# Routing attention and a gelu feed-forward block: another way to load and turn the first pair of heads

## The chip, the cores and the metric

The kernel runs on one core of a Trainium2 chip. The core has TensorE (matmuls, called PE in the profile, with its weight loads as PEld), VectorE (DVE), ScalarE (ACT), GpSimd (POOL), and SyncE (SP), which here only issues transfers; ACT can issue transfers too. The metric is device time in microseconds (us), the median of several runs. Lower is better.

## What is computed

The reference is an attention in which a query sees only the keys of its own cluster, followed by a feed-forward block. Its core:

```python
# q, k, v: (4, 8, 768, 64); centroids: (8, 16, 64)
q_assign = np.argmax(np.einsum('bhsd,hcd->bhsc', q_n, c_n), axis=-1)
k_assign = np.argmax(np.einsum('bhsd,hcd->bhsc', k_n, c_n), axis=-1)
mask = q_assign[:, :, :, None] == k_assign[:, :, None, :]
scores = scale * np.matmul(q, k.transpose(0, 1, 3, 2))
scores = np.where(mask, scores, -1000000000.0)
...                                   # softmax over the keys -> attn
attn_out = np.matmul(attn, v)
...                                   # (B, H, S, D) -> x of (B*S, H*D) = (3072, 512)
h = x @ w_in                          # (512, 2048)
g = h * (1.0 / (1.0 + np.exp(-1.702 * h)))
return (g @ w_out).astype(np.float32)
```

The index `_n` means divided by its own length. For an argmax over centroids the length of q or k does not matter, so the kernel divides only the centroids.

## The kernel before

The attention goes over 16 pairs of heads, (batch, two heads) each. With two heads of 64 features, one pair fills the 128 partitions. A pair `p` has q (`w = 0`) and k (`w = 1`). Each must lie in SBUF with the features on the partitions, as a tile `T[p, w]` of 128 x 768, before scores can be made. The function `prep_turn` makes `T`, `prep_near` multiplies it with the centroids (`cT`, both heads of the pair side by side in 32 columns), `prep_assign` finds the best centroid of every token, and then a mask is added to the scores as a second small matmul (`part`): for pairs from 1 on, one row of codes per head, which `prep_spread` sends through DRAM into `rows_of`; for pair 0, one-hot rows `hots`, made on the chip by `prep_hot`.

Pair 0 and the other pairs take different ways through these functions:

- Loading (`load_qk`). Pair 0: one transfer per head, token `128 j + p` on partition `p`, each piece the 64 features of a token, 256 bytes. Other pairs: a head is loaded in two transfers of 32 features each, pieces of 128 bytes, 32 partitions per transfer, so that 32 x 32 blocks of the tile need only be transposed in place. All are issued by SP.
- Turning (`prep_turn`). Pair 0: twelve transposes on TensorE (L329) by an identity matrix into PSUM, three to a bank, and four copies by ACT (L334). Other pairs: one block transpose of 128 x 768 on VectorE for each of q and k (L322).
- Products with the centroids (`prep_near`). Pair 0: four matmuls of 384 columns, each into 32 partitions of one PSUM bank (L355), then a copy by ACT to SBUF (L361). Other pairs: eight matmuls of 192 columns (L343), which stay in PSUM.
- Assignment (`prep_assign`). Pair 0: three transposes on TensorE (L369). Other pairs: one block transpose on VectorE inside the PSUM bank (L366). Then, for both, a maximum over the 16 centroids (L375), a comparison (L378), a product with a rank (L381). Pair 0 takes another maximum (`code`, L387) and compares it with the ranks, which gives the one-hot tile `hot` (L389).
- Mask operands. Pair 0 (`prep_hot`): twelve small transposes on TensorE (L433), then `hots[0]` is copied from PSUM by VectorE (L438) and `hots[1]` by ACT, as `FAR * x - FAR` (L440).

The order on each engine is the order of the program text, which is written out by hand (a manual schedule). TensorE's filler matmuls on the identity, `keep_busy(n)` at L291, whose result nobody reads, stand between the steps of the start: six before the centroids are transposed (L298), three after `prep_near(0)`, six after the scores of the first two units, four after `prep_hot`. The main loop then goes over steps `t` of two units: scores (L467), mask (L481 for pair 0, L490 for others), exponentials on ACT (L498), sums on GpSimd (L516), values (L532). In step 0, behind the first scores, stand `prep(0, 6)`, which is `prep_hot(0)`, and then the first `part`. Pair 1's q is transposed by VectorE between `prep_assign(0)` and `prep_hot(0)` in VectorE's order, its k right after.

On SP's queue, in order: q and k of pair 0 (four transfers), q of pair 1 (four, L134), v of pair 0 (L144), k of pair 1 (four), a block of weights (L170), q of pair 2, and so on. The tiles of q and k come from a pool of three buffers (`inp`), so k of pair 1 has to wait until q of pair 0 has been turned. Eight completion semaphores serve the transfers in rotation, so a transfer also waits until the one that had its semaphore before has landed. ACT issues the load of the centroids (L151) and no other transfer until the end of the kernel.

After the attention come the feed-forward block (lines from 760 on) and its stores, which the change does not touch.

Of the kernel before, what the change touches and what calls it, by code (L numbers as in the profile page):

```python
# [9 lines left out]
BF16 = mybir.dt.bfloat16  # L10
# [28 lines left out]
def fast(  # L39
# [26 lines left out]
    nc = tc.nc  # L66
# [46 lines left out]
    def bank():  # L113
        return ps_m.tile([P, 512], FP32, name="m")

    def short():
        return tmp.tile([P, HALF], FP32, name="short")
# [4 lines left out]
    def load_qk(p, w):  # L122
        t = inp.tile([P, NJ, 2, D], FP32, name="in")
        b, hp = divmod(p, HP)
        for a in range(2):
            src = (q, k)[w][b, 2 * hp + a]
            if p == 0:
                nc.sync.dma_start(
                    out=t[:, :, a, :],
                    in_=src.rearrange("(j p) d -> p j d", p=P))  # L130
                continue
            for e in range(D // SQ):
                r = a * D + e * SQ
                nc.sync.dma_start(  # L134
                    out=t[r:r + SQ].rearrange("p j a d -> p (j a d)")
                    .rearrange("p (n d) -> p n d", d=SQ),
                    in_=src.rearrange("(n t) d -> t n d", t=SQ)[
                        :, :, e * SQ:(e + 1) * SQ])
        qk_in[p, w] = t
# [177 lines left out]
    def prep_turn(p, i):  # L317
        w, h = divmod(i, 2)
        if h == 0:
            T[p, w] = pairs.tile([P, S], FP32, name=f"T{w}")  # L320
            if p > 0:
                nc.vector.transpose(  # L322
                    out=T[p, w],
                    in_=qk_in[p, w].rearrange("p j a d -> p (j a d)"))
        if p > 0:
            return
        ps = bank()
        for n in range(NH):
            nc.tensor.transpose(out=ps[:, n * P:(n + 1) * P],  # L329
                                in_=qk_in[p, w][:, h * NH + n].rearrange(  # L330
                                    "p a d -> p (a d)"),
                                identity=ident)
        dst = T[p, w][:, h * HALF:(h + 1) * HALF]
        nc.scalar.copy(dst, ps[:, 0:HALF])  # L334

    def prep_near(p):


        ps = bank()
        if p > 0:  # L340
            for w in range(2):
                for r in range(0, P, SQ):
                    nc.tensor.matmul(  # L343
                        out=ps[r:r + SQ, w * NJ * SQ:(w + 1) * NJ * SQ]
                        .rearrange("p (j t) -> p j t", t=SQ),
                        lhsT=cT[:, p % HP].rearrange("p a c -> p (a c)"),
                        rhs=T[p, w].rearrange("d (j t) -> d j t", t=P)[
                            :, :, r:r + SQ],
                        start=True, stop=True)
            sT[p] = ps  # L350
            return
        for w in range(2):
            for h in range(2):
                r = 32 * (2 * w + h)
                nc.tensor.matmul(  # L355
                    out=ps[r:r + 32, 0:HALF],
                    lhsT=cT[:, p % HP].rearrange("p a c -> p (a c)"),
                    rhs=T[p, w][:, h * HALF:(h + 1) * HALF],
                    start=True, stop=True)
        sT[p] = short()  # L360
        nc.scalar.copy(sT[p], ps[:, 0:HALF])  # L361

    def prep_assign(p):
        ps = bank()
        if p > 0:
            nc.vector.transpose(out=ps[:, 0:HALF], in_=sT.pop(p)[:, 0:HALF])  # L366
        else:
            for n in range(NH):
                nc.tensor.transpose(out=ps[:, n * P:(n + 1) * P],  # L369
                                    in_=sT[p][:, n * P:(n + 1) * P],  # L370
                                    identity=ident)
        n = NJ * 4
        sc = ps[:, 0:n * NC].rearrange("p (n c) -> p n c", c=NC)
        best = asg.tile([P, n], FP32, name="best", bufs=1)
        nc.vector.tensor_reduce(out=best, in_=sc, axis=AX.X, op=ALU.max)  # L375
        eq = sc if p > 0 else short().bitcast(BF16)[:, 0:n * NC].rearrange(
            "p (n c) -> p n c", c=NC)
        nc.vector.tensor_tensor(  # L378
            out=eq, in0=sc, in1=best[:, :, None].broadcast_to((P, n, NC)),
            op=ALU.is_equal)  # L380
        nc.vector.tensor_tensor(  # L381
            out=eq, in0=eq, in1=rank[:, None, :].broadcast_to((P, n, NC)),
            op=ALU.mult)
# [15 lines left out]
        turned = ps[:, HALF:HALF + SQ]  # L399
        nc.vector.transpose(out=turned, in_=codes)  # L400
        row = code[p] = asg.tile([P, 2, SQ], BF16, name="row")
        nc.vector.tensor_copy(out=row[:, 0], in_=turned)
        nc.vector.scalar_tensor_tensor(
            out=row[:, 1], in0=turned, scalar=1.0 / CODE, in1=row[:, 0],
            op0=ALU.mult, op1=ALU.mult)
# [17 lines left out]
    def prep_hot(p):  # L423


        rows = slice(0, 2 * SQ)
        for w in range(2):
            hots[w] = hp1.tile([P, S], BF16, name=f"hots{w}")
            ps = bank().bitcast(BF16)
            for h in range(2):  # L430
                for n in range(NH):
                    at = (h * NH + n) * P
                    nc.tensor.transpose(  # L433
                        out=ps[rows, at:at + P],
                        in_=hot_w(w, h, n), identity=ident_h)
            dst = hots[w][rows, :]
            if w == 0:
                nc.vector.tensor_copy(out=dst, in_=ps[rows, 0:S])  # L438
            else:
                nc.scalar.activation(out=dst, in_=ps[rows, 0:S], func=AF.Copy,  # L440
                                     scale=FAR, bias=-FAR)

    def hot_w(w, h, n):
        j = ((n * 2 + w) * 2 + h) * 2
        return hot[:, j:j + 2, :].rearrange("p a c -> p (a c)")

    PREP = [lambda p, i=i: prep_turn(p, i) for i in range(4)]
# [1054 lines left out]
```

## Time and profile before

| | us |
|---|---|
| median of 3 runs (lowest to highest) | 911.01 (910.65 to 911.41) |
| the profiled execution, its own time | 910.43 |
| its span, first to last instruction | 908.5 |
| TensorE busy in the span | 888.4 |
| VectorE busy | 728.6 |
| GpSimd busy | 492.1 |
| ACT busy | 363.3 |

The page cuts the span into 40 slices of 22.7 us. Each digit is a busy share in tenths; the DMA row is the busy share of the 16 DMA engines, and GB/s what they moved:

```profile
PE   8999999999999999999999999999999999999994
DVE  4999999998899997998998556797556797557894
ACT  3777767777676773322111222112222112222110
PEclk9999999999999999999999999999999999999998
DMA  9465556666665210036213202322202322200323
```

The first slice is the only one but the last in which TensorE is not almost fully busy, and the one in which the transfers take the most of the DMA engines. A busy TensorE need not run at its peak: the page models the ends of matmuls. Engines other than TensorE may be idle without a cost.

### The profile page before, as it was taken

Reading aid. Unit: us, or ns where it says so; the run is one execution under the profiler, and the core shown is the slowest. Engines: PE = TensorE matmul, PEld = TensorE weight load, DVE = VectorE, ACT = ScalarE, POOL = GpSimd, SP = SyncE. Lnnn points to the kernel's source line nnn. Section 1 sums busy time; section 2 is a strip of 40 time slices with the busy share of each in tenths; the row PEclk is TensorE's granted clock in tenths of the full one; section 3 lists DMA queues with packets and bytes.
Section 4 is the critical chain, followed back from the end, with each engine's and each line's share of the span. In section 5 each row is a group of like instructions: output and inputs, shape, how many; then the busy total and the mean of one; then the engine's idle time right before and its main releaser. Section 6 shows DMA issues by size and latency. Waiting matters only on the chain.

```text
span 908.5 us, 17741 instructions
## 1 busy us (share of the span) xinstructions
PE 888.4 (98%) x6712; PEld 577.7 (64%) x6712; DVE 728.6 (80%) x1170; ACT 363.3 (40%) x816; POOL 492.1 (54%) x469
## 2 busy tenths in 40 slices
PE   8999999999999999999999999999999999999994
PEld 3344444444444445557996557997557997557994
DVE  4999999998899997998998556797556797557894
ACT  3777767777676773322111222112222112222110
POOL 5899989998999998693274221243221243220220
PEclk9999999999999999999999999999999999999998
DMA  9465556666665210036213202322202322200323
GB/s 176 117 131 107 102 119 129 146 136 132 132 132 122 85 43 18 0 117 232 70 53 109 48 1 70 103 74 90 48 1 70 105 70 93 47 1 1 105 75 69
DMA packets 178397, 78.97 MB, mean 87 GB/s; under 512 B 155272, under 2 KB 161536, under 8 KB 178304
## 3 DMA queue, kind: packets, MB, share of 16 engines
q1 hardware_dynamic: 176912, 77.53, 35.4%
q8 instruction: 55, 0.90, 0.5%
q10 hardware_dynamic: 1392, 0.23, 0.2%
q14 instruction: 38, 0.31, 0.1%
HBM read 61.03 MB, written 16.70 MB: 86 GB/s over the span
## 4 chain that ended last, share of the span: by engine, by line
PE 81%; DVE 9%; DMA 3%; issue 2%; SPq 2%; ACT 2%; POOL 0%; DVEq 0%; ACTq 0%
PE b L845 32%; PE b L895 23%; PE s L467 11%; PE o L532 9%; PE m L549 3%; PE s L490 2%; DVE G L593 2%; DMA raw<-in_moe_w_out_dram 2%; DVE E L593 1%; ACT A L498 1%; SPq L418 1%; DVE Tx L593 1%; PE m L343 1%; DMA line<-row 1%; DVE x L570 1%
## 5 line engine op out<-in xcount | busy, mean ns | idle before, releaser
L516 POOL TENSOR_TENSOR sum<-sum,A 128x384 f32<-128x384 f32 x252 | 264.0, 1082 | 35.8 <-ACT A L498 22.6
L836 DVE TENSOR_TENSOR G<-b,G 128x384 f32<-128x384 f32 x224 | 123.0, 556 | 99.2 <-PE b L845 89.4
L498 ACT ACTIVATE A<-s 128x768 f32<-128x768 f32 x192 | 144.7, 803 | 93.9 <-PE s L490 73.8
L593 POOL TENSOR_TENSOR Y<-y,Y 128x768 f32<-128x768 f32 x28 | 67.4, 2422 | 175.0 <-DVE y L836 151.0
L467 PE MATMUL s<-T,T 64*64 64x384 f32 x1536 | 144.5, 491 | 2.7 <-ACT A L498 0.9
L850 ACT ACTIVATE G<-G 128x384 f32<-128x384 f32 x128 | 66.3, 523 | 198.9 <-DVE G L836 197.6
L532 PE MATMUL o<-A,inv 64*64 64x384 f32 x1536 | 141.3, 483 | 0.0
L593 POOL TENSOR_TENSOR W<-w_in 128x256 f32<-128x256 f32 x32 | 23.6, 736 | 164.2 <-PE b L845 163.8
L593 DVE TENSOR_TENSOR G<-G 128x768 f32<-128x768 f32 (+1 forms) x92 | 104.1, 1156 | 0.0
L467 PEld LDWEIGHTS s<-T,T 64*64 64x64 f32 x1536 | 52.0, 132 | 79.1 <-ACT A L498 52.0
L845 PE MATMUL b<-Tx,w_in 128*128 128x384 f32 x256 | 93.0, 486 | 0.0
L845 PE MATMUL b<-x,W 128*128 128x384 f32 x256 | 93.0, 486 | 0.0
L845 PE MATMUL b<-x,w_in 128*128 128x384 f32 x256 | 88.6, 486 | 0.0
L532 PEld LDWEIGHTS o<-A,inv 64*64 64x64 f32 x1536 | 58.7, 133 | 38.2 <-issue 33.3
L845 PEld LDWEIGHTS b<-x,W 128*128 128x128 f32 x256 | 48.6, 190 | 33.9
L845 PEld LDWEIGHTS b<-Tx,w_in 128*128 128x128 f32 x256 | 48.6, 190 | 33.9
L845 PEld LDWEIGHTS b<-x,w_in 128*128 128x128 f32 x256 | 48.5, 190 | 33.5 <-issue 0.6
L895 PE MATMUL b<-G,w_out 128*128 128x192 f32 x320 | 55.9, 326 | 0.0
L895 PEld LDWEIGHTS b<-G,w_out 128*128 128x128 f32 x320 | 52.7, 190 | 1.1
L895 PE MATMUL b<-E,Wz 128*128 128x192 f32 x288 | 51.5, 328 | 1.4 <-DVE E L593 1.4
L895 PEld LDWEIGHTS b<-E,Wz 128*128 128x128 f32 x288 | 47.1, 190 | 3.4 <-POOL Wz L593 1.3
L845 PE MATMUL b<-Tx,W 128*128 128x384 f32 x128 | 46.6, 487 | 1.5 <-DVE Tx L593 1.5
(169 smaller groups left out, 1357.5 us busy)
## 6 DMA issues: line engine op xcount, KB each, us to landing
Wz<-kept_w SPq DMA_DIRECT2D x78, 256.0 KB
raw<-in_moe_w_in_dram SPq DMA_DIRECT2D x16, 512.0 KB
raw<-in_moe_w_out_dram SPq DMA_DIRECT2D x16, 512.0 KB
inv<-in_v_dram SPq DMA_DIRECT2D x16, 384.0 KB
in<-in_q_dram SPq DMA_DIRECT2D x60, 96.0 KB
in<-in_k_dram SPq DMA_DIRECT2D x60, 96.0 KB
kept<-x SPq DMA_DIRECT2D x24, 192.0 KB
x<-kept SPq DMA_DIRECT2D x24, 192.0 KB
```

The lines of the kernel that those rows point to most:

```text
L343: nc.tensor.matmul(out=ps[r:r + SQ, w * NJ * SQ:(w + 1) * NJ * SQ] .rearrange("p (j t) -> p j t", t=SQ), lhsT=cT[:, p % HP].rearrange("p a ...
L467: nc.tensor.matmul(out=ps[c:c + D, a, 0:HALF], lhsT=T[p, 1][rows, kt * P + c:kt * P + c + D], rhs=T[p, 0][rows, h * HALF:(h + 1) * HALF], ...
L490: nc.tensor.matmul(out=s_of[u][c:c + D, a, :], lhsT=rows_of[1, p % 2][rows, kt * P + c:kt * P + c + D], rhs=rows_of[0, p % 2][rows, h * HA ...
L498: nc.scalar.activation(out=A_of[u], in_=s_of.pop(u), func=AF.Exp, scale=SCALE)
L516: nc.gpsimd.tensor_tensor(out=sum_of[g][:, a], in0=(A_of[u - 1] if kt == 1 else sum_of[g])[:, a], in1=A_of[u][:, a], op=ALU.add)
L532: nc.tensor.matmul(out=o_of[g][a * D:(a + 1) * D, r, 0:HALF], lhsT=v_in[p][rows, a, kt, :], rhs=A[rows, a, :], start=(kt == 0), stop=(kt = ...
L549: nc.tensor.matmul(out=ps[a * D:(a + 1) * D, 0:HALF], lhsT=twos, rhs=sm[:, a, :], start=(i == 0), stop=(i == len(parts) - 1))
L593: engine.tensor_tensor(out=o, in0=a, in1=b, op=(ALU.add if op == "+" else ALU.subtract))
L836: nc.vector.tensor_tensor(out=o, in0=p, in1=a, op=ALU.add)
L845: nc.tensor.matmul(out=ps[:, 0:HALF], lhsT=a[:, c], rhs=x(c), start=(c == 0), stop=(c == 1))
L850: nc.scalar.activation(out=g, in_=g, func=AF.Gelu_apprx_sigmoid, scale=2.0)
L895: nc.tensor.matmul(out=ps, lhsT=A[n][:, f], rhs=M[n][:, f], start=start and f == 0, stop=(f == FQ - 1), skip_group_check=True)
```

## The change

For pair 0, the special way is taken out and the way of the other pairs is used:

- `load_qk` loads pair 0 in 128-byte pieces too, four transfers for q and four for k. Those of k are issued by ACT, those of q by SP.
- `prep_turn(0, .)` is one block transpose on VectorE for q and one for k.
- `prep_near(0)` is the eight matmuls of 192 columns, and their result stays in PSUM.
- `prep_assign(0)` transposes on VectorE inside the bank, and the comparison and the product with the rank are written to PSUM as 32-bit numbers instead of SBUF as bf16.
- `prep_hot` first makes all twelve transposes, then copies in two column halves: `hots[0]` by ACT, `hots[1]` by VectorE (before: `hots[0]` whole by VectorE, `hots[1]` whole by ACT). `hot_w` picks the columns in the order in which they now lie.

The fillers and the order of the steps are as before.

```diff
     def load_qk(p, w):
...
         for a in range(2):
             src = (q, k)[w][b, 2 * hp + a]
-            if p == 0:
-                nc.sync.dma_start(
-                    out=t[:, :, a, :],
-                    in_=src.rearrange("(j p) d -> p j d", p=P))
-                continue
             for e in range(D // SQ):
                 r = a * D + e * SQ
-                nc.sync.dma_start(
+                (nc.scalar if p == 0 and w else nc.sync).dma_start(
                     out=t[r:r + SQ].rearrange("p j a d -> p (j a d)")
                     .rearrange("p (n d) -> p n d", d=SQ),
...
     def prep_turn(p, i):
...
-            if p > 0:
-                nc.vector.transpose(
-                    out=T[p, w],
-                    in_=qk_in[p, w].rearrange("p j a d -> p (j a d)"))
-        if p > 0:
-            return
-        ps = bank()
-        for n in range(NH):
-            nc.tensor.transpose(out=ps[:, n * P:(n + 1) * P],
-                                in_=qk_in[p, w][:, h * NH + n].rearrange(
-                                    "p a d -> p (a d)"),
-                                identity=ident)
-        dst = T[p, w][:, h * HALF:(h + 1) * HALF]
-        nc.scalar.copy(dst, ps[:, 0:HALF])
+            nc.vector.transpose(
+                out=T[p, w],
+                in_=qk_in[p, w].rearrange("p j a d -> p (j a d)"))
...
     def prep_near(p):
...
-        for w in range(2):
-            for h in range(2):
-                r = 32 * (2 * w + h)
-                nc.tensor.matmul(
-                    out=ps[r:r + 32, 0:HALF],
-                    lhsT=cT[:, p % HP].rearrange("p a c -> p (a c)"),
-                    rhs=T[p, w][:, h * HALF:(h + 1) * HALF],
-                    start=True, stop=True)
-        sT[p] = short()
-        nc.scalar.copy(sT[p], ps[:, 0:HALF])
...
     def prep_assign(p):
         ps = bank()
-        if p > 0:
-            nc.vector.transpose(out=ps[:, 0:HALF], in_=sT.pop(p)[:, 0:HALF])
-        else:
-            for n in range(NH):
-                nc.tensor.transpose(out=ps[:, n * P:(n + 1) * P],
-                                    in_=sT[p][:, n * P:(n + 1) * P],
-                                    identity=ident)
+        nc.vector.transpose(out=ps[:, 0:HALF], in_=sT.pop(p)[:, 0:HALF])
...
-        eq = sc if p > 0 else short().bitcast(BF16)[:, 0:n * NC].rearrange(
-            "p (n c) -> p n c", c=NC)
+        eq = sc
...
     def prep_hot(p):
...
-            dst = hots[w][rows, :]
-            if w == 0:
-                nc.vector.tensor_copy(out=dst, in_=ps[rows, 0:S])
-            else:
-                nc.scalar.activation(out=dst, in_=ps[rows, 0:S], func=AF.Copy,
-                                     scale=FAR, bias=-FAR)
+            hot_ps[w] = ps
+        for h in range(2):
+            cols = slice(h * HALF, (h + 1) * HALF)
+            nc.scalar.copy(hots[0][rows, cols], hot_ps[0][rows, cols])
+            nc.vector.tensor_scalar(
+                out=hots[1][rows, cols], in0=hot_ps[1][rows, cols],
+                scalar1=FAR, scalar2=-FAR, op0=ALU.mult, op1=ALU.add)
 
     def hot_w(w, h, n):
-        j = ((n * 2 + w) * 2 + h) * 2
+        j = (w * NJ + h * NH + n) * 2
```

In the program that comes out, the same order holds as in the text: ACT issues the centroids' load, then k's four transfers (the fourth waits for the centroids' semaphore), then loads its function table; SP issues q's four transfers and then, each when its semaphore comes free, the four for q of pair 1. The waits of k of pair 1 are now for VectorE, which turns q of pair 0, instead of TensorE.

More of the change, by code (lines that the diff above doesn't have):

```diff
@@ L333, in prep_turn @@
-        dst = T[p, w][:, h * HALF:(h + 1) * HALF]
-        nc.scalar.copy(dst, ps[:, 0:HALF])
+            nc.vector.transpose(
+                out=T[p, w],
+                in_=qk_in[p, w].rearrange("p j a d -> p (j a d)"))
     def prep_near(p):
         ps = bank()
-        if p > 0:
-            for w in range(2):
-                for r in range(0, P, SQ):
-                    nc.tensor.matmul(
-                        out=ps[r:r + SQ, w * NJ * SQ:(w + 1) * NJ * SQ]
-                        .rearrange("p (j t) -> p j t", t=SQ),
-                        lhsT=cT[:, p % HP].rearrange("p a c -> p (a c)"),
-                        rhs=T[p, w].rearrange("d (j t) -> d j t", t=P)[
-                            :, :, r:r + SQ],
-                        start=True, stop=True)
-            sT[p] = ps
-            return
@@ L352, in prep_near @@
         for w in range(2):
-            for h in range(2):
-                r = 32 * (2 * w + h)
+            for r in range(0, P, SQ):
                 nc.tensor.matmul(
-                    out=ps[r:r + 32, 0:HALF],
+                    out=ps[r:r + SQ, w * NJ * SQ:(w + 1) * NJ * SQ]
+                    .rearrange("p (j t) -> p j t", t=SQ),
                     lhsT=cT[:, p % HP].rearrange("p a c -> p (a c)"),
-                    rhs=T[p, w][:, h * HALF:(h + 1) * HALF],
+                    rhs=T[p, w].rearrange("d (j t) -> d j t", t=P)[
+                        :, :, r:r + SQ],
@@ L359, in prep_near @@
                     start=True, stop=True)
-        sT[p] = short()
-        nc.scalar.copy(sT[p], ps[:, 0:HALF])
+        sT[p] = ps
     def prep_assign(p):
         ps = bank()
-        if p > 0:
-            nc.vector.transpose(out=ps[:, 0:HALF], in_=sT.pop(p)[:, 0:HALF])
-        else:
-            for n in range(NH):
-                nc.tensor.transpose(out=ps[:, n * P:(n + 1) * P],
-                                    in_=sT[p][:, n * P:(n + 1) * P],
-                                    identity=ident)
+        nc.vector.transpose(out=ps[:, 0:HALF], in_=sT.pop(p)[:, 0:HALF])
@@ L423, in prep_hot @@
     def prep_hot(p):
-        rows = slice(0, 2 * SQ)
+        rows, hot_ps = slice(0, 2 * SQ), {}
         for w in range(2):
```

## The prediction

> **What bounds the kernel now.** I read the page first, for the bound of the whole, then the chain of waits and the timeline over the first 18 us, because everything that the diff touches runs once, at the start, and last the busy table by stretches for the pace of the transfers. The page's chain, by engine, and its PE row:
>
> ```profile
> PE 888.4 (98%) x6712; PEld 577.7 (64%) x6712; DVE 728.6 (80%) x1170; ACT 363.3 (40%) x816; POOL 492.1 (54%) x469
> PE 81%; DVE 9%; DMA 3%; issue 2%; SPq 2%; ACT 2%; POOL 0%; DVEq 0%; ACTq 0%
> ```
>
> TensorE is the chain. From 17 to 57 us the chain holds TensorE alone, without a wait, so a start that is later by x us makes the end later by x, and one that is earlier gives x back. The chain of waits over the start (start us, us, what):
>
> ```profile
> 5.50 2.98 PE m L329 x12
> 8.49 2.06 PE m L355 x8
> 10.54 0.75 PE o L291 x3
> 11.30 0.37 PE m L369 x3
> 11.66 1.45 PE s L467 x16
> 13.11 1.40 PE o L291 x6
> 14.52 0.82 PE m L433 x12
> 15.33 0.97 PE o L291 x4
> 16.30 0.29 PE s L481 x2
> ```
>
> The mark I follow is 16.30, where the first masked scores of pair 0 (L481) start. Before it stand the twelve transposes of pair 0 (L329), its products with the centroids (L355), filler matmuls (L291), the scores (L467), and the turning of the one-hot rows (L433). The timeline of the same stretch (start us, us, engine line ...):
>
> ```profile
> 1.63 2.74 PE L291 MATMUL o<-ident_h 128*128 128x512 bf16 x6 [1.63 <-DVE ident_h L245]
> ...
> 13.05 1.47 PE L291 MATMUL o<-ident_h 128*128 128x512 bf16 x6
> ...
> 14.34 0.97 DVE L322 STREAM_TRANSPOSE T<-in 128x768 f32<-128x768 f32 x1
> ...
> 15.37 0.80 ACT L440 ACTIVATE hots<-m 64x768 bf16<-64x768 bf16 x1 [4.31 <-PE m L433]
> ```
>
> The same six fillers take 2.74 us at 1.63 and 1.47 us at 13.05: TensorE starts at about half pace (2.74/1.47 = 1.86). In the trace's clock record the full clock is granted at 10.4 us, 5.36 us after TensorE resumed at 5.06. The busy table by stretches (us, then busy time of the five engines, granted clock, DMA share, GB/s):
>
> ```profile
> 3.00:4.00 1.00, 1.00 (x4) 0.19 (x2) 0.39 (x2) 0.00 (x0) 0.49 (x1) 1.00 1.20 269
> 6.00:7.00 1.00, 1.00 (x5) 0.58 (x5) 0.00 (x0) 0.48 (x1) 0.94 (x2) 1.00 1.55 135
> 44.00:45.00 1.00, 1.00 (x20) 0.56 (x16) 1.00 (x2) 0.17 (x1) 1.00 (x2) 1.00 1.05 168
> ```
>
> At 3 us the 256-byte pieces of pair 0 arrive at 269 GB/s; at 6 us the 128-byte pieces of pair 1, queued without a gap, at 135; at 44 us pieces of 128 bytes again, at 168. The trace's completion records agree: q of pair 0 has landed at 4.69, k at 6.81, q of pair 1 at 9.81. So 393 KB cost 2.12 us in the old form and 3.00 us in the new.
>
> **The change, part by part.** *Loads.* Pair 0 goes from 2 x 1536 pieces to 2 x 3072. The stream of q began, by these numbers, at 4.69 - 2.12 = 2.57. SP issues q's four DMAs from 0.74, ACT issues k's four behind the centroids' issue (0.43 us), so q has 0.43 us alone. I take the two queues to share one pace, 3.00 us for each tensor. Then q needs 0.43 + 2 x 2.57 = 5.57 and lands at 8.14. k has 0.43 us of work left, and shares again, with q of pair 1, which SP sends behind q: 0.86, so 9.00. Bounds from rows of single queues, since no row shows both queues loading: fastest, each queue runs at 168 GB/s unhindered, 2.34 us for a tensor, q at 4.9, k at 5.3; slowest, the pace of the 256-byte pieces of v (9.81 to 11.74, 1.93 us for 1536 pieces, so 3.86 us a tensor), q at 9.86, k at 10.72. The 128-byte load right behind these loads is the nearest row, so 3.00. The fourth k DMA waits for the centroids' semaphore (landed 2.92) and costs nothing; the table load of ACT (1.28 us) now stands behind these issues and is done long before ACT's first operation.
>
> [...]
>
> *Blocks on VectorE.* Two transposes of 0.97 us (the row at 14.34) replace 12 TensorE transposes and 4 ACT copies. VectorE is free from 6.0. The one of q runs 8.19 to 9.17, the one of k 9.17 to 10.15. Call this last time N; after it TensorE has, at full clock by the chain, half of the products of L343's form (the other pairs' 0.79 us, so 0.40; the half of q ran before N), three fillers 0.75, the scores 1.45, six fillers 1.40: 4.00 us. But TensorE is idle from 5.5 to 9.2, had not reached the full clock by then, and starts this work at half pace: 0.74 + 1.37 + 2.71 + 2.74 = 7.56 (each by the factor 1.86 or from the 2.74 us row). The clock comes up w after 9.17. I take w = 5.36, the measured time from resumption. Then 4.38 us after N run cold and do 58% of the work, the other 42% take 1.68: the one-hot rows are turned from N + 6.06 = 16.21. Bounds of w: 2.0 if only the products of L355 (8.42 to 10.4) count, 8.79 if the count began at 1.63, in which case all 7.56 us run cold.
>
> [...] This trace shows 5.36 with small gaps. [...]
>
> VectorE's chain beside it: near products done at N + 0.74, then transpose 0.63, maximum 0.59, compare 0.60, multiply 0.60, code 0.59, one-hot 0.60, each with its gap from the same operations of pair 1 at 21.79 to 24.81: N + 4.4. TensorE's 6.06 hides it, and so the ACT copy of L361 and the three transposes of L369, which stood in that chain and are gone, bring nothing. At full clock VectorE would end last instead of the fillers, 0.4 us over them. The transpose of q of pair 1 (0.97) stays in front of the one-hot copies; it ends at N + 5.4, and needs q at about 11.6, so N + 1.4: hidden.
>
> *Column halves.* The first half on ACT takes about 0.48 (the 128x384 copies of L334), where 0.80 stood. Nothing is gained: the four fillers behind the turning end at 16.30, the old copy at 16.17. Without the fillers it would be worth 0.3 us. VectorE's two halves, at most 0.51 each (the whole old copy), end within 1.02 us, beside the fillers' 0.97. The new column order in hot_w moves nothing.
>
> *Later loads.* k of pair 1 waits for VectorE's transpose of q (9.17) where it waited for TensorE until 7.05. Its old landing was 14.55; now q of pair 1 lands at 2.57 + 9.0 = 11.6, v at 13.5, k at 16.3. VectorE reaches its transpose after the copies at about 17.5, so it waits for nothing. All SP work behind (weights, the other pairs, the row spread for pair 1) slides by up to 2 us; the spread's last row landed at 32.2 for a use at 36.8, so 4.6 us of cover. If that were gone, every us beyond it would be added once.
>
> **The sum.** From 16.21 on, turning and four fillers, 14.52 to 16.30 before, 1.79: first masked scores at 18.00, against 16.30: +1.70 us, carried to the end. The profiled execution took 910.43 (span 908.5, 1.9 around it), so 912.1; the median of the runs is 0.6 higher, 911.01, so 912.7.
>
> **The rivals.** *Cold all the way:* same loads, w = 8.79, 7.56 us after N: 19.5, +3.2, 914.2. For it: six fillers from 1.63 did not raise the clock; against: 5.36 us later it was up. With the slow loads too (N = 11.87) 21.2, +4.9, 915.9. *Even:* the pieces come at the 168 GB/s of 44 us, shared (q 6.82, k 7.68, N 8.82), with w = 5.36: 16.67, +0.4, 911.4. For it: that row has the same pieces; against: there the queue had gaps, at 6 us it had none, as here. *Faster:* the second queue is a second pace, k is there before VectorE is free, N = 7.95, and the clock comes 2.0 us after resumption: turning at N + 4.5, scores at 14.2, -2.1, 908.9. It decides once N is below about 8.2 with an early clock, and what pays is the 5.0 us of transposes and products at half clock that TensorE no longer does. Against it: TensorE's idle stretch, and two favourable bounds at once. That the change does not do what it says is excluded by the instruction order: the twelve transposes and five copies are gone, k's DMAs stand on ACT.
>
> **How the numbers follow.** Forecast 912.7, with its own range 911.6 to 913.8 (w from 4.3 to 6.5, the middle third of its bounds, which gives 17.5 to 18.5, and the pace a tenth either way, 0.6 us): chance 0.46. Cold all the way, with or without slow loads: 0.25. Even: 0.16. Faster: 0.13. The line is 0.2%, 1.8 us, about what a measurement of this kernel can tell from no change. Half of the forecast's case lies over it (0.22), with all of the cold case: slower 0.47. Faster 0.13, within 0.40. The range 909.6 to 915.0 leaves out the end of the faster case and the cold case with slow loads.
>
> **What would show it.** In the changed kernel's timeline: VectorE's two transposes of pair 0 at about 8.2 and 9.2 (at 6.0 and 7.0 the faster rival has its loads; after 10 the loads were slower); the stretch from 3 to 8 us at about 135 GB/s; the six fillers before the turning near 1.9 us in all, partly cold (2.74 is the cold rival, 1.47 an early clock); masked scores at 18.0; from there the same distances as before. Wrong it would be if the first masked scores move by 1.7 and the span does not, or if a later wait of TensorE is new.

## The result, and the profile after

| | before | changed |
|---|---|---|
| median of 12 runs each (lowest to highest), us | 910.78 (909.79 to 911.42) | 912.58 (911.61 to 913.69) |
| ratio, with its 95% interval | | 1.0020 (1.0013 to 1.0028) |
| profiled execution, its own time / span, us | 910.43 / 908.5 | 912.75 / 911.0 |

The change costs 1.8 us in the medians and 2.3 in the profiled executions. The forecast was 912.7.

The page of the changed kernel has TensorE less busy by 1.6 us, VectorE busier by 3.3, and the share of transfers (DMA) in the chain up from 3% to 5%:

```profile
PE 886.8 (97%) x6705; PEld 575.5 (63%) x6705; DVE 731.9 (80%) x1174; ACT 361.3 (40%) x812; POOL 492.8 (54%) x469
PE 79%; DVE 9%; DMA 5%; issue 3%; SPq 2%; ACT 2%; ACTq 0%; DVEq 0%
```

The chain of waits over the start of the changed kernel (start us, us, what) has a transfer of k in it:

```profile
3.22 5.87 DMA in<-in_k_dram
9.11 0.99 DVE T L316
10.10 0.04 issue
10.14 0.87 PE m L326 x8
11.01 1.39 PE o L286 x3
12.40 2.77 PE s L433 x16
15.17 1.64 PE o L286 x6
16.81 0.79 PE m L398 x12
17.60 0.97 PE o L286 x4
18.57 0.29 PE s L447 x2
...
39.07 0.33 PE s L456 x8
```

In the kernel before, the same chain has, further on than the lines in the prediction:

```profile
36.81 0.32 PE s L490 x8
...
38.42 1.55 PE s L467 x16
```

Before, this chain was TensorE's alone from 5.50 to the first masked scores. Now the last piece of k holds it until 9.09, then VectorE's transpose, and then the same scores that took 1.45 us take 2.77, 1.91 times as long: half clock. The first masked scores stand at 18.57 against 16.30, 2.27 later. The first mask of pair 1 (L456, before L490) stands at 39.07 against 36.81: 20.50 behind, against 20.51. Nothing behind the start gives the 2.27 back: the last matmuls of TensorE's timeline start at 897.14 (L861) against 894.85 (L895), 2.29 later.

The timeline of the changed kernel over the same stretch (start us, us, engine line ..., in brackets the idle time before and what ended it):

```profile
7.59 0.98 DVE L316 STREAM_TRANSPOSE T<-in 128x768 f32<-128x768 f32 x1 [1.31 <-DMA in<-in_q_dram]
8.62 0.87 PE L326 MATMUL m<-T,cT 128*32 128x192 f32 x8 [2.84 <-DVE T L316]
9.11 0.98 DVE L316 STREAM_TRANSPOSE T<-in 128x768 f32<-128x768 f32 x1 [0.54 <-DMA in<-in_k_dram]
...
14.09 0.56 DVE L354 TENSOR_TENSOR hot<-code,rank 128x384 bf16<-128x384 f32 x1
...
15.10 1.71 PE L286 MATMUL o<-ident_h 128*128 128x512 bf16 x6
...
17.63 0.61 DVE L405 TENSOR_SCALAR hots<-m 64x384 bf16<-64x384 bf16 x2 [2.10 <-PE m L398]
```

TensorE stands idle for 2.84 us ahead of 8.62. VectorE has the one-hot tile at 14.65, transposes q of pair 1, and then waits 2.10 us for TensorE at L405: VectorE's chain is hidden, TensorE's is not. The six fillers take 1.71 us, between 2.74 (half clock) and 1.47 (full): the clock came up inside them, at 15.62 by the trace's clock record.

The busy table by stretches of the changed kernel (as before: us, busy time of the five engines, clock, DMA share, GB/s) for the transfers:

```profile
2.00:3.00 1.00, 1.00 (x4) 0.41 (x3) 0.14 (x2) 0.00 (x0) 0.00 (x0) 1.00 1.09 182
3.00:4.00 1.00, 1.00 (x4) 0.19 (x2) 0.45 (x2) 0.00 (x0) 0.21 (x1) 1.00 1.15 172
6.00:7.00 1.00, 0.00 (x0) 0.00 (x0) 0.26 (x2) 0.00 (x0) 0.94 (x2) 1.00 1.59 145
7.00:8.00 1.00, 0.00 (x0) 0.00 (x0) 0.41 (x1) 0.00 (x0) 0.94 (x2) 1.00 1.60 138
```

At 6 to 8 us both queues together move 145 and 138 GB/s, where in the kernel before one queue with the same pieces moved 135 at 6 us and the old pieces 269 at 3 us. The completion records give q at 7.47 (before 4.69) and k at 9.08 (before 6.81).

One subtraction sorts this: from k's landing to the first masked scores on the timeline (0.06 ahead of the chain's mark) pass 16.24 - 6.81 = 9.43 us before and 18.50 - 9.08 = 9.42 after. All the work behind k has been rebuilt, and in these two executions it takes as long as it did. The whole shift is as long as k's delay, 2.27. That the two times agree to 0.01 us is chance, as the experiments show: the work behind k got shorter, and more of it ran at half clock, until 15.62 instead of 10.41.

### The profile page after: what moved, and what is told of

It is laid out like the page before. It is cut to its first block, busy times and chain, and to the rows that moved or that the text cites. A ratio compares the mean times of both kernels' runs of the same rounds, so it can differ in the third digit from the quotient of the medians.

```text
span 911.0 us, 17734 instructions
## 1 busy us (share of the span) xinstructions
PE 886.8 (97%) x6705; PEld 575.5 (63%) x6705; DVE 731.9 (80%) x1174; ACT 361.3 (40%) x812; POOL 492.8 (54%) x469
## 4 chain that ended last, share of the span: by engine, by line
PE 79%; DVE 9%; DMA 5%; issue 3%; SPq 2%; ACT 2%; ACTq 0%; DVEq 0%
PE b L811 32%; PE b L861 23%; PE s L433 10%; PE o L498 8%; PE m L515 2%; PE s L456 2%; DVE G L559 2%; DMA raw<-in_moe_w_out_dram 2%; ACT A L464 1%; SPq L383 1%; DVE E L559 1%; DMA line<-row 1%; PE m L326 1%; DVE Tx L559 1%; DMA raw<-in_moe_w_in_dram 1%
## 5 line engine op out<-in xcount | busy, mean ns | idle before, releaser
L433 PE MATMUL s<-T,T 64*64 64x384 f32 x1536 | 145.8, 495 | 2.8 <-ACT A L464 1.4
L433 PEld LDWEIGHTS s<-T,T 64*64 64x64 f32 x1536 | 52.3, 132 | 80.6 <-ACT A L464 52.5
L861 PE MATMUL b<-G,w_out 128*128 128x192 f32 x320 | 55.9, 326 | 0.0
L861 PEld LDWEIGHTS b<-G,w_out 128*128 128x128 f32 x320 | 52.7, 190 | 1.1
L861 PE MATMUL b<-E,Wz 128*128 128x192 f32 x288 | 51.5, 328 | 1.4 <-DVE E L559 1.4
L861 PEld LDWEIGHTS b<-E,Wz 128*128 128x128 f32 x288 | 47.1, 190 | 3.4 <-POOL Wz L559 1.3
```

The source lines that it names most:

```text
L433: nc.tensor.matmul(out=ps[c:c + D, a, 0:HALF], lhsT=T[p, 1][rows, kt * P + c:kt * P + c + D], rhs=T[p, 0][rows, h * HALF:(h + 1) * HALF], ...
L861: nc.tensor.matmul(out=ps, lhsT=A[n][:, f], rhs=M[n][:, f], start=start and f == 0, stop=(f == FQ - 1), skip_group_check=True)
```

## The experiments

The theory after this reading: the 128-byte pieces make k late, and turning on VectorE does save TensorE time, but the idle TensorE then works at half clock for so long that the saving is eaten. Its rivals: that the second queue is at fault, that VectorE's turning is worth nothing in itself, and that the column halves take part. Each edit is against the changed kernel unless it says "before". The times "before" were taken beside each group of runs.

All of them in one view. Marks are from each profile, in us: k landed, full clock there to stay, first masked scores, and the time between k and these. The column "median - before" is the difference of the medians. The ratio and its interval are not the quotient of these two medians (e1: 911.11 / 910.36 would be 1.0008, and the ratio is 1.0016); what is called apart below is apart by the interval.

| kernel | k | clock | masked | k to masked | median - before | ratio (95%) |
|---|---|---|---|---|---|---|
| before | 6.81 | 10.41 | 16.24 | 9.43 | | |
| changed | 9.08 | 15.62 | 18.50 | 9.42 | +1.80 | 1.0020 (1.0013 to 1.0028) |
| e5 pieces only | 8.45 | 13.76 | 18.60 | 10.15 | +1.98 | 1.0020 (1.0011 to 1.0029) |
| e2 one queue | 8.46 | 15.05 | 17.91 | 9.45 | +1.63 | 1.0021 (1.0012 to 1.0029) |
| e1 gap filled behind the centroids | 8.94 | 9.71 | 15.99 | 7.05 | +0.75 | 1.0016 (1.0005 to 1.0027) |
| e4 six fillers out | 8.98 | 15.02 | 16.76 | 7.78 | +0.64 | 1.0011 (1.0002 to 1.0020) |
| e3 halves only | 6.84 | 9.40 | 15.73 | 8.89 | +0.01 | 1.0001 (0.9992 to 1.0010) |
| f1 all gaps filled | 8.87 | 6.79 | 15.91 | 7.04 | +0.49 | 1.0006 (0.9995 to 1.0018) |
| f2 the same, one queue | 8.16 | 6.46 | 15.20 | 7.04 | +1.69 | 1.0029 (1.0018 to 1.0039) |
| f3 before, gap filled | 7.12 | 4.46 | 15.24 | 8.12 | -0.89 | 0.9994 (0.9985 to 1.0003) |
| g3 pieces only, gaps filled | 8.22 | 6.89 | 16.30 | 8.08 | +1.43 | 1.0011 (1.0001 to 1.0022) |
| g2 = f2, third block of weights early | 8.27 | 5.98 | 15.31 | 7.04 | -0.31 | 0.9998 (0.9989 to 1.0007) |
| g1 = f3, third block of weights early | 6.54 | 5.28 | 14.81 | 8.27 | -1.04 | 0.9989 (0.9980 to 0.9998) |

A profile is one execution, and the clock came at another place in nearly every one of them, so a mark and a median can differ by some tenths; where they differ by more, it is said.

### The load form alone (e5)

The kernel before, with pair 0 still turned by TensorE, but each head loaded in two transfers of 128-byte pieces:

```diff
             if p == 0:
-                nc.sync.dma_start(
-                    out=t[:, :, a, :],
-                    in_=src.rearrange("(j p) d -> p j d", p=P))
+                for e in range(0, D, SQ):
+                    nc.sync.dma_start(
+                        out=t[:, :, a, e:e + SQ],
+                        in_=src.rearrange("(j p) d -> p j d", p=P)[
+                            :, :, e:e + SQ])
                 continue
```

> The kernel before with one part of the change alone: q and k of pair 0 are loaded in 128-byte pieces, on SP's queue, into the same place as before, and TensorE turns them as before. If 128-byte pieces cost 3.0 us a tensor where 256-byte pieces cost 2.12: q lands at about 5.6 instead of 4.69, k at about 8.6 instead of 6.81. TensorE turns q from 5.6 and then waits for k until 8.6, where it stood at 6.95: the first masked scores move by about 1.7 us, less what an earlier clock gives back on the rest (up to 0.9): 911.6 to 912.6 against 910.8 before. If the form of the pieces is hidden or free, nothing moves, 910.8, and the whole cost of the change lies in the turning on VectorE and in the clock.

Measured: 912.34 against 910.36, ratio 1.0020, the ratio of the whole change. Its chain of waits (start us, us, what):

```profile
5.04 3.42 DMA in<-in_k_dram
8.45 0.09 issue
8.54 1.51 PE m L331 x6
10.06 2.06 PE m L357 x8
...
18.67 0.29 PE s L483 x2
```

The last six of the twelve transposes, those of k, now wait for the transfer; before they ran without a wait. k is 1.64 later than before and the masked scores 2.36: the other 0.7 is put down to the clock, which came at 13.76 instead of 10.41, 5.3 us behind k instead of 3.6, after a stretch in which TensorE waited. So the load form by itself costs what the whole change costs; what the rest of the change adds and saves can't be seen beside it in the time.

### The second queue (e2)

```diff
-                (nc.scalar if p == 0 and w else nc.sync).dma_start(
+                nc.sync.dma_start(
```

> The changed kernel with all eight loads of pair 0 on SP's queue, q first. If both queues share one pace (3.0 us for each tensor in 128-byte pieces): q has landed at about 5.6, k at about 8.6 instead of 9.08, both block transposes stand earlier (k's ends at 9.6 instead of 10.1), TensorE resumes at about 7.3 instead of 8.62 and its clock comes earlier by up to 1.3: first masked scores 0.5 to 1.2 us earlier, 911.4 to 912.1. If the second queue brings a pace of its own: k lands later than 9.1, 0 to 0.6 us slower, 912.6 to 913.2.

Measured: 911.99, ratio 1.0021. Against the change's 1.0020 no difference can be seen. In the trace q lands at 5.70 instead of 7.47 and k at 8.46 instead of 9.08, so the second queue makes both later: all transfers of q and k, and those of pair 1's q behind them, then share one pace. From 2 to 9 us the two queues move as much as the one (the last column is GB/s; changed kernel, then e2):

```profile
2.00:9.00 7.00, 3.20 (x15) 0.99 (x13) 2.88 (x12) 1.28 (x1) 4.95 (x7) 1.00 1.44 158
2.00:9.00 7.00, 3.21 (x15) 0.90 (x13) 3.39 (x13) 0.47 (x1) 5.08 (x8) 0.94 1.28 157
```

In the five profiles with 128-byte pieces on one queue (e2, e5, f2, g2, g3) k landed between 8.16 and 8.46, in the four with two queues (changed, e1, e4, f1) between 8.87 and 9.08. The chain of the changed kernel starts with k's fourth transfer, issued at 3.22 when the centroids' semaphore came; but e2 issues its last transfer of k at 4.71 and has k earlier, so this wait isn't what makes k late. Both queues together move 145 GB/s from 6 to 7 us and 138 from 7 to 8, beside 135 of one queue in the kernel before and 148 of one in e2 (both from 6 to 7 us): no pace of its own shows for the second queue.

### TensorE's gap and its clock (e1, e4, f1)

e1 fills the gap between the centroids' transpose and the first products with seven fillers:

```diff
     nc.tensor.transpose(out=cps[:, 0:P], in_=cc.rearrange("p a d -> p (a d)"),
                         identity=ident)
+    keep_busy(7)
```

> The changed kernel with seven more filler matmuls right behind the transpose of the centroids, so that TensorE works from 5.8 to about 8.8 us, where it stood idle. Theory 1 (TensorE starts the new chain at half clock, and the full clock comes late, at 15.6 us in the changed kernel's profile): the clock comes by about 11 to 12, VectorE's chain then ends last, the one-hot rows are turned at about 14.6 and the first masked scores stand at 16.4 to 16.8 instead of 18.57: 1.8 to 2.2 us less, about 910.6. Theory 2 (the late k sets the start, the clock is immaterial): nothing moves, 912.6. Theory 3 (VectorE's longer chain of operations): nothing moves either.

Measured: in the profile the clock is up at 9.71 instead of 15.62, the masked scores stand at 15.99, 7.05 behind k instead of 9.42. The mechanism is there: in this execution 2.4 us between k and the masked scores hung on the clock. In the time it is less clear. The median, 911.11, is 0.75 over the kernel before, but the interval of the ratio (1.0005 to 1.0027) overlaps the change's, and the profiled execution is 0.25 ahead of the kernel before at the mark. The runs spread from 909.27 to 914.60, the widest of the changed versions; the kernel before, in the 27 runs beside g1 to g3, spreads as wide (908.85 to 914.32). A gap is left at 4.4 to 5.2 us and one of 0.6 ahead of k's products. Why the long runs are long was not seen, since only one execution has a profile. Their mean granted clock is known: 0.993 in the two longest (914.27 and 914.60), 0.995 or 0.996 in the ten others. This mean leaves out the time ahead of the first clock record (the changed kernel's profile has 0.996, though its full clock came at 15.62), so the lower mean is more time at half clock behind the first grant, not a first grant that came late. It doesn't settle the cause: the kernel before has a run of 910.73 with 0.993 too.

e4 leaves the six fillers ahead of the turning out instead:

```diff
         if t == 0:
-            keep_busy(6)
             prep(0, 6)
```

> The changed kernel without the six filler matmuls between the first scores and the turning of the one-hot rows. Theory 1 (TensorE at half clock ends last there): the turning starts when the scores end, at about 15.2 instead of 16.8; with the clock coming at about 15.6 it stays partly cold, so the first masked scores gain 1.2 to 1.6 us: 911.0 to 911.4. Theories 2 and 3 (late k, or VectorE's chain, sets the turning): nothing moves, 912.6.

Measured: 911.00, +0.64, ratio 1.0011 (1.0002 to 1.0020). The turning starts at 15.00 instead of 16.74 and the masked scores come 1.74 earlier. In the kernel before these fillers cover the wait for `hot` (ready at 14.42, fillers until 14.52). In the changed kernel they start at 15.10, when `hot` is ready already (14.65), and the first half us of them runs at half clock.

f1 fills all gaps: eight fillers instead of six ahead of the centroids' transpose, seven behind it, two between the products of q and of k.

```diff
-    keep_busy(6)
+    keep_busy(8)
     cps = bank()
     nc.tensor.transpose(out=cps[:, 0:P], in_=cc.rearrange("p a d -> p (a d)"),
                         identity=ident)
+    keep_busy(7)
...
         for w in range(2):
+            if p == 0 and w:
+                keep_busy(2)
             for r in range(0, P, SQ):
```

What the expectations of f1 and f3 call a grid is this: in e2 the granted clock changes at 4.81, 8.23 and 15.05, in e4 at 4.78, 8.19 and 15.02, so 3.41 us or twice that apart.

> The changed kernel with TensorE filled from 1.6 us on: eight fillers instead of six before the transpose of the centroids, seven behind it, two between the products of q and those of k. [...] Theory 1 (clock): without gaps every place of the grid gives the full clock by 8.5 us, so in all runs, not only in the profiled one, the first masked scores stand near 16.0, 2.5 us before the changed kernel's 18.57: 910.4 against 912.6, and the spread of the runs is no wider than the changed kernel's. Theory 2 (late k alone): 912.6 in the median.

Measured: 910.78, ratio 1.0006 (0.9995 to 1.0018): of the change's 1.8 us some 0.5 is left in the medians; the interval holds nothing as well as nearly the whole of the change. The full clock by 8.5 us in all runs was the author's estimate; the one profile has it at 6.79. That its runs would spread no wider than the changed kernel's did not come true: 909.34 to 913.32, 4.0 us against 2.1. Its chain of waits:

```profile
9.92 0.58 PE m L329 x8
10.52 0.61 DVE m L340
...
13.54 0.57 DVE hot L357
14.11 0.04 issue
14.15 0.86 PE m L401 x12
...
32.59 3.92 DMA raw<-in_moe_w_in_dram
36.54 0.80 ACT w_out L226 x2
```

Two things are to be seen. With the clock up, VectorE's assignment (L340 to L357) is the chain, not TensorE. And a transfer stands in it that was in neither main kernel's chain at this place: ACT waits 0.72 us for the third block of weights (`raw`) at 36.5. The masked scores are 0.33 ahead of the kernel before; the scores behind this wait start at 38.93 against 38.42, 0.51 behind. So 0.84 is lost there.

### The column halves (e3)

The kernel before, with `prep_hot` as in the change:

```diff
-            if w == 0:
-                nc.vector.tensor_copy(out=dst, in_=ps[rows, 0:S])
-            else:
-                nc.scalar.activation(out=dst, in_=ps[rows, 0:S], func=AF.Copy,
-                                     scale=FAR, bias=-FAR)
+            hot_ps[w] = ps
+        for h in range(2):
+            cols = slice(h * HALF, (h + 1) * HALF)
+            nc.scalar.copy(hots[0][rows, cols], hot_ps[0][rows, cols])
+            nc.vector.tensor_scalar(
...
```

> The kernel before with the column halves alone: the one-hot rows are copied in two halves, those of q by ACT, those of k by VectorE. All theories: the four fillers behind the turning cover the copy either way (old copy ready at 16.17, fillers done at 16.30), so nothing moves by more than 0.2 us: 910.4. A rival in which the copy ends last would give 0.3 us less, 910.1.

Measured: 910.30 against 910.29, ratio 1.0001 (0.9992 to 1.0010). The halves show no worth. The mark in its profile is 0.5 earlier, but its clock came 1.0 earlier too (9.40), and a clock that is earlier by 1 us lets about 0.5 us go at half pace (six fillers: 2.74 us against 1.47): the clock explains it without the halves. The new column order in `hot_w` is not in this run, nor alone in any other.

### What an earlier start is worth (f2, f3, g3, g1, g2)

Three kernels take the gap away in other settings. f2: f1's idea on one queue, with 8, 3 and 6 fillers. f3: the kernel before with 8 fillers instead of 6 ahead of the centroids' transpose. g3: e5 with 8, and four between the transposes of q and those of k.

f2, beside the one queue of e2:

```diff
-    keep_busy(6)
+    keep_busy(8)
...
+    keep_busy(3)
...
+            if p == 0 and w:
+                keep_busy(6)
```

> The same, with all loads of pair 0 on SP's queue: eight fillers before the transpose of the centroids, three behind it, six between the products of q and of k. k landed 0.5 us earlier in that form (block transpose ended at 9.47 instead of 10.1). Theory 1: VectorE's chain ends last, 4.2 us behind the transpose of k, so the rows are turned at 13.7 and the first masked scores stand at about 15.5: 0.8 us under the kernel before, 909.6 to 910.2. If the clock does not come without the long work behind the loads, 17.9 and 912.

f3, against the kernel before:

```diff
-    keep_busy(6)
+    keep_busy(8)
```

> The kernel before with eight fillers instead of six before the transpose of the centroids, so that its own gap of 0.7 us at 4.4 is closed. Theory 1 (clock on a grid): the full clock comes by 8.5 us at the latest instead of 8.5 to 11.9 (10.4 in its profile); the transposes and products that run cold today until 10.4 shrink, but q of pair 0 is there at 4.7 and k at 6.8, so up to 1 us is saved: 909.5 to 910.4 against 910.4. If the clock did not count: 910.4, no change.

g3, beside the edits of e5 and f3:

```diff
     for p, i in [(0, i) for i in range(6)] + [(1, i) for i in range(2)]:
+        if (p, i) == (0, 2):
+            keep_busy(4)
         prep(p, i)
```

> The kernel before with 128-byte pieces for pair 0, turned by TensorE, and with TensorE filled from 1.6 us on (eight fillers before the transpose of the centroids, four between the transposes of q and those of k). With the pieces alone k's transposes started at 8.54 and the first masked scores stood at 18.6. Theory 1: with the full clock up by 8.5 us the rest after k's landing shrinks from 10.2 us to about 7.5 to 8, masked scores at 16.1 to 16.6, 910.3 to 911. Then the turning on VectorE (15.9 in the changed kernel without gaps) is worth 0.2 to 0.7 us at full clock. Rival (the turning on TensorE costs the same at any clock): 18 and more, 912.

Measured. f2 has its masked scores at 15.20, 1.04 ahead of the kernel before, and yet a median 1.69 over it. f3 has them at 15.24 and gains 0.89 in the median, 0.9994 (0.9985 to 1.0003), which can't be told from nothing. g3 has them at 16.30, as late as the kernel before, and is 1.43 slower. In all three ACT waits for the third block of weights at 36 to 38 us; f3's chain shows it:

```profile
31.89 3.82 DMA raw<-in_moe_w_in_dram
35.73 0.80 ACT w_out L231 x2
```

The block lands at 35.2 in the kernel before, whose ACT asks for it at 36.05 and finds it. In f3 it lands at 35.7, and ACT, earlier by the earlier start, waits 0.58. What each loses there can be read from two marks of its chain against the kernel before, the first masked scores and the scores behind the wait (38.42 in the kernel before):

| us against the kernel before | f1 | f3 | f2 | g3 |
|---|---|---|---|---|
| first masked scores | -0.33 | -1.00 | -1.04 | +0.06 |
| scores behind the wait | +0.51 | -0.30 | +0.31 | +1.90 |
| lost between | 0.84 | 0.70 | 1.35 | 1.84 |

g3's 912.02, where its expectation had 910.3 to 911, is this loss. f2's median is not explained by it alone: behind its last matmuls 0.7 us more pass than in the kernel before, and four of its nine runs (912.75 to 914.58) lie over an us above the profiled one.

These profiles also price VectorE's turning: with the clock up before k lands, k to masked scores takes 7.04 where VectorE turns (f1, f2, and g2 below) and 8.08 to 8.27 where TensorE turns (f3, g3, and g1 below). VectorE's way is worth 1.0 to 1.2 us in these profiles; f2 and g3, which load in the same pieces on the same queue, give 1.0.

g1 is f3 and g2 is f2, each with the third block issued in step 0 behind the turning of pair 1, which puts it ahead of the spread of pair 1's rows on SP's queue instead of behind it:

```diff
     def rounding():
         i = w_done[0]
-        load_w(i + 2)
+        if i:
+            load_w(i + 2)
...
         for p, i in turns:
             prep(p, i)
+        if t == 0:
+            load_w(2)
```

> The kernel before with the closed gap (eight fillers before the transpose of the centroids) and with the third block of weights loaded before the row spread of pair 1 on SP's queue instead of behind it. In the profile of the kernel with the closed gap alone, the first masked scores came 1.06 us earlier than before, but 0.75 us of it was lost at 36 us, where ACT waits for that block. If that wait was the loss, the block lands by about 29, the start's gain is kept and the median is 909.3 to 909.7 against 910.3; if the row spread, now behind the block, takes the wait's place, it is 910.3 or more.

> The changed kernel with one queue, without gaps on TensorE, and with the third block of weights before the row spread. Without the last part its first masked scores stood at 15.2 in the profile (16.24 before, 18.5 changed), but 1.5 us were lost at 36 us, where ACT waits for the block behind a queue full of 128-byte pieces, and the median was 912.0. If that wait is what is left of the late loads: masked scores at 15.2, no wait at 36 us, 909.3 to 910.2. If the loads stay late elsewhere (pair 1's rows, the other blocks): 911 to 912.

Measured: g1 909.55 against 910.59, ratio 0.9989 (0.9980 to 0.9998): faster than the kernel before and than the change. SP's timeline shows the block where it was put, at 25.38 ahead of the spread (L413, L419), with landing at 29.7:

```profile
25.38 0.52 SPq L170 DMA_DIRECT2D raw<-in_moe_w_in_dram  x1
26.00 1.58 SPq L413 DMA_DIRECT2D line<-row  x4
31.53 2.31 SPq L419 DMA_DIRECT2D rows<-line  x8
33.95 0.84 SPq L170 DMA_DIRECT2D raw<-in_moe_w_in_dram  x2
```

In ACT's timeline the first pass over that block then starts at 34.62 without a wait. g1 and f3 are not apart by their intervals. For g2 the same edit takes 1.0029 (1.0018 to 1.0039) to 0.9998 (0.9989 to 1.0007), apart by their intervals. So the wait for the block was real and cost f2 a large part of its loss. In the profiles the same scores start at 59.41 in f2 and at 58.46 in g2, 0.95 earlier, though g2's first masked scores are 0.11 later; the spans differ by 1.7 (909.7 and 908.1), and the rest of that lies behind the last matmuls and has no explanation here. g2 also has a new wait: the block stands ahead of the spread, and so the rows of pair 1 are now just too late. Its chain:

```profile
34.93 1.25 DMA rows<-line
...
36.27 0.51 PE s L460 x6
```

This first mask of pair 1 is 20.89 behind g2's first masked scores (15.38 in the chain), where it is 20.51 behind in the kernel before: 0.4 is lost. g1 has its 20.51.

g2 against g1 is the changed way against the old one with both mended: 0.9998 against 0.9989, with overlapping intervals. Run against run, taken side by side, they are clearer: the medians are 910.28 and 909.55, and eight of g1's eleven runs lie under the fastest of g2 (909.88). In the profile k lands 1.73 later in g2 and the turning takes 1.23 less: 0.5 remains (15.31 against 14.81), and the wait for the rows adds 0.4. The new way, as far as it was mended here, doesn't earn back its load.

## Why the prediction was right, step by step

- *Loads.* k was put at 9.00 and landed at 9.08; that both queues share one pace held (158 GB/s, one queue 157). That k fits to 0.08 is in part luck. The pace was quicker than the 3.00 us for a tensor (2.76 from q to k in e2), and the queues did not share evenly: q, put at 8.14, landed at 7.47, when k still had a whole transfer and part of another to come (7.96 and 9.08), where the sum had one seventh of a tensor left. Nothing hung on q, since VectorE then waited for k (0.54 us).
- *Blocks on VectorE.* N was 10.15, measured 10.09. TensorE resumed at 8.62, not at 9.17.
- *The clock.* This is the term that was mis-sized. w, the time from TensorE's resumption to the full clock, was taken as the 5.36 of the old trace. With it the full clock would have come at 14.53; it came at 15.62, 7.0 after resumption. 1.09 us more at half pace leave 0.55 us of work over, and the turning began at 16.74 instead of 16.21, the masked scores at 18.57 instead of 18.00. So w lay within the bounds 2.0 and 8.79, but outside the 4.3 to 6.5 from which the forecast's own range was made, and the mark just outside its 17.5 to 18.5. The reasoning under the term did not hold either: from resumption to the full clock passed 5.36 us in the kernel before and 7.0 in the changed one, so the old trace's 5.36 did not carry over, and what the clock goes by was not shown (last section).
- *VectorE's chain.* N + 4.4 was forecast, 4.56 measured, hidden behind TensorE as said. That at full clock VectorE would end last came true in e1, f1 and f2.
- *Column halves, the new order in `hot_w`.* The halves show no worth in e3, as said; the order was in no run by itself.
- *Later loads.* VectorE's transpose of k of pair 1 starts at 18.17 with no wait, and the distance to pair 1's mask is the old one; the cover held. In the other direction it did not: the prediction did not look at what an earlier start would meet, and its faster rival (-2.1) would have come to the third block of weights at 36 us as f1, f2 and f3 did.
- *The sum.* +1.70 at the mark, measured +2.27; the medians differ by 1.80. That the forecast of 912.7 meets 912.58 is in part luck: the mark's shift was a third larger than forecast, the profile of one execution stands over the median difference by 0.5, and the base, 911.01 from three runs, is 910.78 over twelve.
- *The rivals.* The cold rival came nearest in kind: of the 7.56 us that TensorE's work between N and the turning would take at half clock, 5.53 us (10.09 to 15.62), 73%, ran so, where the forecast had 58%. But the clock came before the end. The even and faster rivals wanted faster loads, and neither queue gave them.

## What to carry to other kernels

When a step is moved off the bottleneck engine, see first which landing gates it, and what the new form does to that landing: here halved pieces took 1.65 us (e2 against the kernel before) and a second queue 0.4 to 0.9 more, against a saving of about 1 us. Where TensorE no longer works at the start, see at which pace the work behind it runs: in the changed kernel the scores took 2.77 us instead of 1.45 and the saving was gone, and with the gaps filled (f1) the time from k to the masked scores fell from 9.42 to 7.04. And an earlier start is worth something only as far as the next transfer that is just in time (f3 lost 0.70 of its 1.00 us at the third block of weights); find that one and issue it earlier in the same edit, and see what it then stands ahead of (in g2, the rows of pair 1).

## What the runs showed of the hardware

*The clock.* e2 was granted the full clock at 4.81, lost it at 8.23 and had it back at 15.05; e4 at 4.78, 8.19 and 15.02. The changes lie 3.41 us or twice that apart. Over the 13 profiles the first grant falls at other places, from 4.46 (f3) to 15.62 (changed kernel). From TensorE's resumption to the full clock passed 5.36 and 7.0 us in the two main traces. e2's busy table, cut at its changes and in steps of 3.41 us:

```profile
1.40:4.81 3.41, 2.74 (x6) 0.73 (x6) 1.69 (x14) 1.07 (x1) 1.21 (x3) 1.00 0.91 147
4.81:8.23 3.42, 0.83 (x9) 0.29 (x9) 1.77 (x6) 0.00 (x0) 3.17 (x6) 1.00 1.40 150
8.23:11.64 3.41, 2.12 (x11) 0.49 (x11) 2.12 (x3) 0.00 (x0) 3.20 (x5) 0.50 1.48 170
11.64:15.05 3.41, 3.41 (x19) 1.08 (x19) 3.15 (x6) 0.00 (x0) 1.78 (x3) 0.50 1.45 160
```

The first column of times is TensorE's: 2.74 of 3.41 us busy ahead of the first grant, 0.83 ahead of the loss, 2.12 ahead of a stretch that is still at half clock (0.50), 3.41 ahead of the grant that stays. In the last stretch, at 0.50, the scores (L433) take 2.84 us, where they take 1.45 in the kernel before. The 1.00 in the clock column of the first line isn't a full clock, since matmuls there take the 2.74 us that six fillers take at half pace: ahead of its first record the column shows 1.00.

Other profiles were cut the same way, in steps of 3.41 us back from a grant. The last stretch ahead of the grant that stays was busy throughout in the kernel before, the changed kernel, e3, e4, e5, f1, f2 and g1; it was busy for 3.25 us in g3, 3.10 in e1 and 2.83 in f3. A stretch with 2.74 us was followed by a grant in e2 and e4, one with 2.76 by none in the changed kernel and in e3, one with 2.72 by none in the kernel before. So the busy time, in which the ends of matmuls are modelled, does not separate the two, and what the clock goes by was not shown. The six fillers from 1.63 us on were followed by a grant at 4.81 in e2 and by none before 15.62 in the changed kernel. Whether such differences make e1's wide spread (909.27 to 914.60) wasn't shown either, and f1, with its gaps filled, spreads nearly as wide (909.34 to 913.32).

*The smaller pieces took longer.* Between the landings of q and of k, 393 KB apart on one queue, lay 2.12 us in pieces of 256 bytes (kernel before; 1.92 to 2.30 in e3, f3 and g1) and 2.76 in pieces of 128 bytes (e2: 5.70 and 8.46; 2.72 to 2.77 in e5, f2, g2 and g3). The number of bytes is the same and the number of pieces twice as large.
